# Attention followed by a squared-ReLU feed-forward layer: the tokens of layer one's second half in reverse order, the ReLU moved to layer two's reads, and x's sums moved up in GpSimd's queue

## The chip, the cores and the metric

One core of one Trainium2 chip. The metric is the device time of one launch in microseconds (us), median of several runs.

## The reference

Attention over 8 batches and 12 heads (448 positions, 64 wide) with RMS-normalised q and k gives x, 3584 tokens by 768. Then the feed-forward layer:

```python
h = x @ w_in                 # 3584 x 768 by 768 x 2048: layer one
r = np.maximum(h, 0.0)
g = s * (r * r) + b
return (g @ w_out).astype(np.float32)    # 3584 x 2048 by 2048 x 768: layer two
```

w_in and w_out come as 64-bit floats and are turned into 32-bit ones on the chip. All outputs are 32-bit floats.

## The kernel before

The kernel has three parts that follow each other: attention (up to 548 us in the profile), layer one (548 to 1028 us) and layer two (from 1033 us). The program writes the order of each engine's instructions by hand: what is emitted first on an engine runs first on it, and an instruction that waits holds up all that is behind it on its engine. The sync engine's queue (SP) issues nearly all DMAs of the two layers, in the same way. Data dependences, and buffers that are used again, are guarded by semaphores that the framework puts in.

Both layers multiply by a seven-product scheme on two-by-two blocks (`MUL`), and each 32-bit operand is split in a rounded part and a remainder, so that one product takes three multiplies. So each operand needs *sums* of its four quarters (`s_sums` for x, `sums_right` for w_out, `g_sums` for g: additions on GpSimd, POOL in the profile) and a *split* (`split`: a copy on ScalarE, ACT, then a subtraction on VectorE, DVE, lines 149 and 151).

**Layer one.** A block is one group of 512 tokens (seven groups, `NG`) times one of eight column groups of w_in (`q`). Four column groups fit in SBUF at a time, so there are two halves: `runs` lists seven groups of tokens with columns 0 to 3, then seven with columns 4 to 7. A run is four blocks (i = 0 to 3), and there are 14 runs, 56 blocks. A block is 63 multiplies into four PSUM banks (`ffn_in`, line 478). As there are eight banks, a block can start when the block two before it has been read out. x's three tiles (k = 0, 1, 2) of the next run are made during the present one:

- `s_load`: a load from DRAM of k = 0 and 1 in block i = 0, of k = 2 in block i = 2, into two buffers in turn;
- `s_sums` (lines 137 to 139): k = 0 and 1 in block i = 1, k = 2 in block i = 2;
- `s_split`: k = 0 in block i = 1, the two others in block i = 3.

In each block the order of emission is: the block's multiplies, `s_load`, the load of a piece of w_out (`convert_out`), `rectify` of the block before, the rest of the w_out conversion that was begun a block earlier (`finish(x)`: four DVE instructions, one on ACT, and, every second time, three sums on POOL and a store to `w_d`), and then `steps`: x's sums and splits, and loads and splits of weights. `rectify` adds up the seven products: four ACT copies and eight DVE additions out of PSUM (lines 487 to 492), a ReLU on ACT over 128 x 1024 (line 522), and a store to `r_d`. The w_out pieces are put together in one buffer (`o9`), free again when its store to `w_d` has landed.

At the turn between the halves (blocks 24 to 32) the columns 4 to 7 of w_in are loaded (`tin_load`, six buffers) and split (`tin_split`, 12 times, the subtraction on POOL), while x's tiles of token group 0 are loaded and made once more.

**Layer two.** 112 rounds of 21 multiplies (`multiply`, line 643). Each round reads a piece of `r_d` back (`g_load`), squares it on ACT (line 605, 128 x 512), scales it on DVE, makes the sums on POOL and DVE, and splits it (ACT line 627, DVE line 628), two to three rounds ahead of its multiplies. Eight rounds make 256 tokens, and `combine` adds the products up. The first rounds also need w_out's last splits (`tout_load`, `tout_split`). Between the layers the last block is rectified.

Of the kernel before, what the change touches and what calls it, by code (L numbers as in the profile page):

```python
# [12 lines left out]
AF = mybir.ActivationFunctionType  # L13
# [32 lines left out]
def attention_then_relu2_ffn(  # L46
# [13 lines left out]
    V, S, G, T = nc.vector, nc.scalar, nc.gpsimd, nc.tensor  # L60
# [82 lines left out]
    def t_in(q):  # L143
        if q not in tin:
            tin[q] = wpool.tile([P, NK, 2, 7, P], F32R, tag=f"s{q % QUADS}", name=f"tin{q}")
        return tin[q]

    def split(to, of, E=V):
        S.copy(to[0], of)  # L149
        yield  # L150
        E.tensor_tensor(to[1], of, to[0].bitcast(F32), ALU.subtract)  # L151
# [284 lines left out]
    s9s, sns = {}, {}  # L436

    def s_load(n):
        g, k = divmod(n, NK)
        g %= NG  # L440
        t = s9s[n] = pools["s9", n % 2].tile([P, 9, 2 * P], F32, tag="s9", name=f"s9_{n}")
        t0 = TG * g
        while t0 < TG * (g + 1):
            b, off = divmod(t0, SEQ)
            w = min(TG * (g + 1) - t0, SEQ - off)
            o = t0 - TG * g
            nc.sync.dma_start(
                four(t, 2 * P)[:, :, o : o + w],
                x_d[b][2 * k : 2 * k + 2, :, off : off + w].rearrange("f p t -> p f t"),
            )  # L450
            t0 += w

    def s_sums(n):
        sums_right(s9s[n], G)
# [7 lines left out]
    def finish(g):  # L462
        for _ in g:
            pass
# [2 lines left out]

    hs, rfirst = {}, []

    def ffn_in(r, q):  # L470

        banks = hs[q] = [psum(f"h{r}_{q}_{i}") for i in range(4)]
        for k in range(NK):
            w, x = t_in(q)[:, k], sns[NK * r + k]
            for j, (sa, tb) in enumerate(MUL):
                to = banks[j // 2][0][:, j % 2 * 2 * P : (j % 2 + 1) * 2 * P]
                for n, (lw, lx) in enumerate(((0, 0), (1, 0), (0, 1))):
                    T.matmul(  # L478
                        to, w[:, lw, sa], x[:, lx, tb],
                        start=k == n == 0 and j % 2 == 0, stop=k == NK - 1 and n == 2,  # L480
                        skip_group_check=True,
                    )
# [23 lines left out]
    def rectify(r, g, q):  # L506

        banks = hs.pop(q)
        if r == 0 or (r, q) == (1, 0):
            if not rfirst:  # L510
                rfirst.append(pools["t4"].tile([P, QUADS + 1, 2 * TG], F32, tag="t0", name="rfirst"))
            rt = rfirst[0][:, QUADS * r + q]
        else:
            rt = lp.tile([P, 2 * TG], F32, tag="uz", bufs=4, name=f"r{g}_{q}")
        c = [rt[:, i * 2 * P : (i + 1) * 2 * P] for i in range(4)]

        def part(j):
            return banks[j // 2][0][:, j % 2 * 2 * P : (j % 2 + 1) * 2 * P]

        add_up(c[3], c[2], c[1], c[0], part)  # L520
        free.extend(bank for _, bank in banks)
        S.activation(rt, rt, AF.Relu)  # L522
        nc.sync.dma_start(
            r_d[q][g].rearrange("f p t -> p f t"), rt.rearrange("p (f t) -> p f t", f=2)
        )
# [13 lines left out]
    def tin_split(n):  # L539
        q, k = divmod(n, NK)  # L540
        to = t_in(QUADS + q)
        return split((to[:, k, 0], to[:, k, 1]), staged[0][:, n % 6], G)

    touts = {}

# [41 lines left out]
    PAIRS = NT // (2 * P)  # L587
    ROUNDS = NM * PAIRS

    raws, g9s, ghs = {}, {}, {}  # L590

    def g_load(x):
        if x >= ROUNDS:
            return
        p, m = divmod(x, NM)
        raw = raws[x] = pools["g"].tile([P, 2, 2 * P], F32, tag="raw2", bufs=3, name=f"raw2_{x}")
        g, o = p // 2, p % 2 * 2 * P
        nc.sync.dma_start(raw, r_d[m][g][:, :, o : o + 2 * P].rearrange("f p t -> p f t"))

    def g_sums(x):  # L600
        if x >= ROUNDS:
            return
        raw = raws.pop(x)
        g9 = g9s[x] = pools["g"].tile([P, 9, P], F32, tag="g9", bufs=2, name=f"g9_{x}")
        S.activation(raw, raw, AF.Square)
        V.tensor_scalar(four(g9, P), raw, sb_s, sb_b, ALU.mult, ALU.add)  # L606
        G.tensor_tensor(  # L607
            g9[:, 2:4], g9[:, 0:2], g9[:, 7:8].broadcast_to([P, 2, P]), ALU.add
        )
        V.tensor_tensor(g9[:, 4], g9[:, 1], g9[:, 8], ALU.add)  # L610
        G.tensor_tensor(g9[:, 5:7], g9[:, 0:9:8], g9[:, 1:8:6], ALU.subtract)  # L611
# [40 lines left out]
    def combine(p):  # L652
        ot = ots[p] = pools["w9"].tile([P, 2, DM], F32, tag="w9", bufs=2, name=f"ot{p}")

        def done(j, h):
            if p == PAIRS - 1:
                t0, c = (2 * p + j) * P, slice(h * HALF, (h + 1) * HALF)
                nc.sync.dma_start(out[t0 : t0 + P, c], ot[:, j, c])

        add_up(  # L660
            ot[:, 1, HALF:], ot[:, 1, :HALF], ot[:, 0, HALF:], ot[:, 0, :HALF],
            lambda j: ms[p, j][0][:, :HALF], done,
        )
        free.extend(ms.pop((p, j))[1] for j in range(7))

    def store(p):
        ot = ots.pop(p)
        for j in range(2):
            t0 = (2 * p + j) * P
            nc.sync.dma_start(out[t0 : t0 + P, :], ot[:, j])  # L670

    def pool(stack, name, side, **of):
# [4 lines left out]
    with tc.manual_schedule(engines=ORDERED):  # L677
# [21 lines left out]
            tc.tile_pool(name="ps", bufs=1, space=PSUM, reuse_waits="tile")  # L699
        )  # L700
        todo = list(range(4 * NM))
        runs = [(g, q0) for q0 in (0, QUADS) for g in range(NG)]
        blocks = [(r, g, q0 + i) for r, (g, q0) in enumerate(runs) for i in range(QUADS)]
        nb = len(blocks)

        def steps(n):

            r, g, q = blocks[n]
            i = q % QUADS
            s0 = NK * (r + 1)  # L710
            if r + 1 < len(runs):
                if i == 1:
                    s_sums(s0)
                    s_sums(s0 + 1)
                    finish(s_split(s0))
                elif i == 2:
                    s_sums(s0 + 2)
                elif i == 3:
                    finish(s_split(s0 + 1))
                    finish(s_split(s0 + 2))  # L720
            b = n - (NG - 1) * QUADS
            if -2 <= b <= 0:
                for k in range(2):
                    tin_load(2 * (b + 2) + k)
            if 0 < b <= QUADS:
                for k in range(NK):
                    finish(tin_split(NK * (b - 1) + k))
                    tin_load(NK * (b + 1) + k)
            if n == nb - 14:
                tout_load(0)  # L730
                tout_load(1)
            if n == nb - 13:
                finish(tout_split(0))
                finish(tout_split(1))
            b = n - (nb - QUADS)
            if b == 0:
                tout_load(2)
                tout_load(3)
            elif b > 0:
                for k in (2 * b, 2 * b + 1):  # L740
                    finish(tout_split(k))
                    tout_load(k + 2)

        for n, (r, g, q) in enumerate(blocks):
            ffn_in(r, q)
            i = q % QUADS
            if r + 1 < len(runs):
                if i == 0:
                    s_load(NK * (r + 1))
                    s_load(NK * (r + 1) + 1)  # L750
                elif i == 2:
                    s_load(NK * (r + 1) + 2)
            begun_, fresh = begun[:], []
            begun.clear()
            if n >= 2 and todo and i != 2 and not 24 <= n < 29:
                c = convert_out(todo.pop(0))
                next(c)
                fresh.append(c)
            if n:
                rectify(*blocks[n - 1])  # L760
            for u in range(3 * n, 3 * n + 3):
                if u < 20:
                    slot(NSLOT + 2 + u)
            for x in begun_:
                finish(x)
            begun.extend(fresh)
            steps(n)
            if n == nb - QUADS - 1:
                assert not todo and not begun
                late.close()  # L770
                pools["g"] = pool(ctx, "gpool", "left")
                for x in range(3):
                    g_load(x)
            if n == nb - 3:
                g_sums(0)
                g_sums(1)
            if n == nb - 2:
                g_load(3)
                g_load(4)
        g_split(0)  # L780
        mid.close()
        pools["t"] = pool(ctx, "tpool", "right")
        g_split(1)
        g_sums(2)
        rectify(*blocks[-1])
        for k in (8, 9):
            finish(tout_split(k))
            tout_load(k + 2)
# [61 lines left out]
```

## Time and profile before

| | |
|---|---|
| median of 3 runs | 1466.35 us (1465.26 to 1466.78) |
| profiled execution | 1465.44 us |
| its span | 1463.7 us |
| PE, busy share of the span | 93% |
| DVE / ACT / POOL | 67% / 52% / 57% |
| mean granted TensorE clock | 0.972 |

The profile was taken of one execution; the span goes from its first to its last instruction, and 1.74 us lie outside of it. PE is TensorE's matrix multiply. A busy PE means that a multiply is under way; in a gap between multiplies it waits for an engine or a transfer. "<-" in a row names what ended the wait just before.

### The profile page before, as it was taken

What the parts mean: (1) busy time and instruction counts of PE and PEld (TensorE: products, weight loads), DVE (VectorE), ACT (ScalarE), POOL (GpSimd) and SP (SyncE); (2) the same over time, 40 slices, a digit from 0 to 9 for tenths busy, and PEclk for the clock granted to TensorE, in tenths of its full rate; (3) what the DMA queues carried; (4) which work ended last, traced back from release to release, by engine and by line L of the source; (5) the groups of instructions that cost most, each with busy time, mean ns of one, the idle gap of its engine ahead of it and who ended that gap; (6) DMA issues with size and microseconds to landing.
All of it is one profiled execution on the core that took longest, in us unless ns stands there. A gap on an engine that the chain in (4) does not pass through costs nothing.

```text
span 1463.7 us, 26101 instructions
## 1 busy us (share of the span) xinstructions
PE 1357.6 (93%) x9760; PEld 1079.9 (74%) x9760; DVE 975.4 (67%) x1534; ACT 766.7 (52%) x1132; POOL 839.2 (57%) x731
## 2 busy tenths in 40 slices
PE   2699999999999999899998899989699999999999
PEld 2344444444444439899988798989699999999998
DVE  3467777766666624676754676777786777677765
ACT  3367777776666653444445444445554444444443
POOL 6357989887878535444458435342265465546553
PEclk6799999999999999999999999999799999999999
DMA  7578888889998635465665465645632233223221
GB/s 199 157 197 227 252 230 231 252 235 265 253 266 255 179 88 158 152 201 168 196 208 180 143 196 172 209 153 203 222 132 96 85 122 95 94 87 123 94 94 65
DMA packets 172366, 253.71 MB, mean 173 GB/s; under 512 B 54544, under 2 KB 122832, under 8 KB 172240
## 3 DMA queue, kind: packets, MB, share of 16 engines
q1 hardware_dynamic: 165904, 231.86, 51.6%
q10 hardware_dynamic: 6336, 20.19, 5.2%
q8 instruction: 76, 1.25, 0.4%
q14 instruction: 50, 0.41, 0.1%
HBM read 183.06 MB, written 68.76 MB: 172 GB/s over the span
## 4 chain that ended last, share of the span: by engine, by line
PE 53%; issue 12%; DMA 11%; POOL 9%; DVE 8%; ACT 4%; SPq 2%; ACTq 0%; POOLq 0%; DVEq 0%
PE m L643 26%; PE av L293 8%; PE st L272 7%; PE av L300 4%; PE sh L243 4%; DVE r L487 3%; PE h L478 3%; DMA s<-x_d 2%; POOL s L139 2%; PE st L276 2%; DVE s L151 2%; DMA to<-w_d 2%; ACT s L149 2%; POOL s L138 1%; POOL s L137 1%
## 5 line engine op out<-in xcount | busy, mean ns | idle before, releaser
L478 PE MATMUL h<-s,tin 128*128 128x256 f32 x3528 | 440.2, 287 | 40.4 <-DVE r L487 19.5
L478 PEld LDWEIGHTS h<-s,tin 128*128 128x128 f32 x3528 | 431.0, 192 | 50.5 <-DVE r L487 24.7
L643 PE MATMUL m<-tout,gh 128*128 128x384 f32 x1568 | 406.3, 340 | 7.4 <-ACT gh L627 7.1
L252 DVE TENSOR_REDUCE nmx<-sh 112x2 fp32r<-112x896 f32 x192 | 209.1, 1091 | 142.4 <-PE sh L243 141.3
L643 PEld LDWEIGHTS m<-tout,gh 128*128 128x128 f32 x1568 | 288.7, 191 | 8.7 <-ACT gh L627 7.7
L643 PE MATMUL m<-tout,gl 128*128 128x384 f32 x784 | 267.2, 341 | 4.7 <-DVE gl L628 4.7
L283 ACT ACTIVATE e<-st 128x896 f32<-128x896 f32 x192 | 177.1, 922 | 118.7 <-PE st L276 118.4
L607 POOL TENSOR_TENSOR g<-g 128x256 f32<-128x256 f32 x112 | 94.5, 844 | 225.1 <-DVE g L606 225.1
L627 ACT CAST gh<-g 128x896 fp32r<-128x896 f32 x112 | 105.4, 942 | 174.7 <-POOL g L611 97.8
L628 DVE TENSOR_TENSOR gl<-g,gh 128x896 fp32r<-128x896 f32 x112 | 137.2, 1226 | 65.0 <-ACT gh L627 64.9
L272 PE MATMUL st<-kqv 64*128 64x448 f32 x768 | 179.9, 545 | 0.0
L151 DVE TENSOR_TENSOR s<-s,s 128x1792 fp32r<-128x1792 f32 x42 | 87.5, 2105 | 130.9 <-ACT s L149 122.7
L293 PE MATMUL av<-e,kqv 128*32 128x448 f32 x1536 | 164.4, 545 | 9.5 <-ACT uz L316 7.0
L643 PEld LDWEIGHTS m<-tout,gl 128*128 128x128 f32 x784 | 149.5, 191 | 6.5 <-DVE gl L628 6.5
L487 DVE TENSOR_TENSOR r<-r,h 128x256 f32<-128x256 f32 x408 | 139.5, 412 | 18.1 <-ACT r L491 17.8
L229 POOL TENSOR_TENSOR kqv<-kqv,rb 128x448 f32<-128x448 f32 x95 | 124.2, 1324 | 38.8 <-ACT kqv L225 13.9
L522 ACT ACTIVATE r<-r 128x1024 f32<-128x1024 f32 x51 | 54.1, 1061 | 173.9 <-DVE r L487 173.9
L202 POOL TENSOR_TENSOR ri<-ri,mhalf 128x14 f32<-128x14 f32 x48 | 141.7, 2951 | 4.0
L243 PEld LDWEIGHTS sh<-kr 64*112 64x112 f32 x384 | 54.3, 277 | 121.4 <-issue 29.5
L276 PE MATMUL st<-shq,row 64*128 64x448 f32 x384 | 139.6, 719 | 3.5 <-DMA shq<-nmx 3.5
L611 POOL TENSOR_TENSOR g<-g 128x256 f32<-128x256 f32 x112 | 133.4, 1191 | 0.0
L243 PE MATMUL sh<-kr 64*112 64x448 f32 x384 | 91.7, 474 | 35.4 <-ACT kr L234 25.3
(78 smaller groups left out, 1584.8 us busy)
## 6 DMA issues: line engine op xcount, KB each, us to landing
kqv<-in_dram SPq DMA_DIRECT2D x48, 704.0 KB
raw<-r_d SPq DMA_DIRECT2D x112, 256.0 KB
r_d<-r SPq DMA_DIRECT2D x51, 512.0 KB
rb<-i_d SPq DMA_DIRECT2D x96, 224.0 KB
raw<-in_dram ACTq DMA_DIRECT2D x44, 448.0 KB
w64i<-in_dram SPq DMA_DIRECT2D x24, 512.0 KB
w64o<-in_dram SPq DMA_DIRECT2D x32, 384.0 KB
uz<-z_d SPq DMA_DIRECT2D x96, 112.0 KB
```

The costliest lines, as they stand in the source:

```text
L202: G.tensor_tensor(ri, ri, mhalf[:, :n], ALU.pow)
L243: T.matmul(sh[:QC, j, :SEQ], t[d, 1].rearrange("k (p c) -> k c p", c=NQ)[:, c], t[d, 0], start=True, stop=True,)
L252: V.tensor_reduce(out=nmxs[p][:, :, c : c + 1], in_=shs.pop(i)[:QC, :, :SEQ], op=ALU.max, axis=AX.X, negate=True,)
L272: T.matmul(st[:, j, :SEQ], t[d, 0, k0 : k0 + P], t[d, 1], start=True, stop=False)
L276: T.matmul(st[:, j, :SEQ], row[d], shq[p % 3][d], start=False, stop=True)
L283: S.activation(e, sts.pop(i)[:, :, :SEQ], AF.Exp)
L293: T.matmul(t[n * Q : (n + 1) * Q, 0, :SEQ], x[:, 2 * g + h, j, m * Q : (m + 1) * Q], e[h][:, j], start=g + h == 0, stop=g + h == 2,)
L478: T.matmul(to, w[:, lw, sa], x[:, lx, tb], start=k == n == 0 and j % 2 == 0, stop=k == NK - 1 and n == 2, skip_group_check=True,)
L487: V.tensor_tensor(to, a, part(j), op_)
L611: G.tensor_tensor(g9[:, 5:7], g9[:, 0:9:8], g9[:, 1:8:6], ALU.subtract)
L628: V.tensor_tensor(gl, g9[:, 1:8], gh.bitcast(F32), ALU.subtract)
L643: T.matmul(to, g[:, sa], w, start=m == 0 and n == 0, stop=m == NM - 1 and n == 2,)
```

## The change

- `runs` takes the second half's token groups backwards (6 to 0), so the last run of the first half and the first of the second use the same tokens. x's tiles are kept from the one to the other (`first_s`, `fresh_x`): 13 sets of x's tiles are made instead of 14, and none during run 6. Layer two and the stores to `out` take the tokens backwards too (`tokens`).
- `rectify` has no ReLU any more; `g_sums` applies it to the 128 x 512 tile that layer two has read, ahead of the square, 112 times.
- `steps` is cut in two: `sums` (x's sums on POOL) stands ahead of `rectify` and of the rest of the w_out conversion; `parts` (splits, weights) stays behind them.
- The subtraction of `tin_split` is on DVE for k = 0 and 1, and on POOL for k = 2 alone.
- One more conversion of w_out is begun in block 28 instead of a later one (`24 <= n < 28`).
- The last block's `rectify` stands ahead of `g_split(1)` and `g_sums(2)`.

```diff
-        g, k = divmod(n, NK)
-        g %= NG
+        u, k = divmod(n, NK)
+        g = min(u, 2 * NG - 2 - u)
...
+    def first_s(r):
+        return NK * (r if r < NG else r - 1)
...
-            w, x = t_in(q)[:, k], sns[NK * r + k]
+            w, x = t_in(q)[:, k], sns[first_s(r) + k]
...
-        S.activation(rt, rt, AF.Relu)
...
-        return split((to[:, k, 0], to[:, k, 1]), staged[0][:, n % 6], G)
+        return split((to[:, k, 0], to[:, k, 1]), staged[0][:, n % 6], G if k == 2 else V)
...
+    def tokens(p):
+        return 2 * (NG - 1 - p // 2) + p % 2
...
+        S.activation(raw, raw, AF.Relu)
         S.activation(raw, raw, AF.Square)
...
-        runs = [(g, q0) for q0 in (0, QUADS) for g in range(NG)]
+        runs = [(g, 0) for g in range(NG)] + [(g, QUADS) for g in reversed(range(NG))]
...
+        def fresh_x(r):
+            return r + 1 < len(runs) and r != NG - 1
+
+        def sums(n):
+
+            r, _, q = blocks[n]
+            if fresh_x(r):
+                for k in {1: (0, 1), 2: (2,)}.get(q % QUADS, ()):
+                    s_sums(first_s(r + 1) + k)
+
+        def parts(n):
+
+            r, _, q = blocks[n]
+            if fresh_x(r):
+                for k in {1: (0,), 3: (1, 2)}.get(q % QUADS, ()):
+                    finish(s_split(first_s(r + 1) + k))
...
-            if n >= 2 and todo and i != 2 and not 24 <= n < 29:
+            if n >= 2 and todo and i != 2 and not 24 <= n < 28:
...
+            sums(n)
             if n:
                 rectify(*blocks[n - 1])
...
-            for x in begun_:
+            for x in last:
                 finish(x)
-            begun.extend(fresh)
-            steps(n)
+            begun.extend(next_)
+            parts(n)
...
+        rectify(*blocks[-1])
         g_split(1)
         g_sums(2)
-        rectify(*blocks[-1])
```

## Rows read from the trace of the kernel before

**Rows 1.** The page's first part: busy us (share of span), instructions.

```profile
PE 1357.6 (93%) x9760; PEld 1079.9 (74%) x9760; DVE 975.4 (67%) x1534; ACT 766.7 (52%) x1132; POOL 839.2 (57%) x731
```

**Rows 2.** Windows, layer one's multiplies by run: stretch, length, busy (count), granted clock.

```profile
548.12:581.58 33.46, 32.54 (x252) 32.33 (x253) 0.92 0.52 153
581.58:617.02 35.44, 31.24 (x254) 30.20 (x253) 1.00 0.51 169
...
684.52:715.77 31.25, 30.82 (x254) 30.20 (x253) 1.00 0.52 171
...
783.21:827.97 44.76, 33.83 (x254) 32.39 (x253) 0.92 0.42 141
...
925.79:964.84 39.05, 32.74 (x254) 31.71 (x253) 0.96 0.62 206
...
692.69:707.64 14.95, 14.95 (x128) 14.95 (x127) 1.00 0.56 193
sum 494.47, PE 455.17 PEld 445.95; mean PE 30.34 PEld 29.73
```

**Rows 3.** Waits in layer one: who waited for whom, us, times, longest.

```profile
POOL o L137 <- DVE o L118: 174.5, 15, 17.7
ACT r L522 <- DVE r L487: 170.1, 50, 5.6
DVE s L151 <- ACT s L149: 101.1, 23, 8.9
ACT s L149 <- POOL s L139: 60.2, 16, 6.5
```

**Rows 4.** Timeline of POOL, run 3: start, us, line, tiles, idle before.

```profile
665.23 1.00 POOL L137 TENSOR_TENSOR o<-o 128x384 f32<-128x384 f32 x1 [13.88 <-DVE o L118]
...
667.71 1.28 POOL L137 TENSOR_TENSOR s<-s 128x512 f32<-128x512 f32 x1
...
672.83 3.06 POOL L139 TENSOR_TENSOR s<-s 128x512 f32<-128x512 f32 x1
```

**Rows 5.** Timeline of DVE, runs 3 and 4.

```profile
660.22 2.74 DVE L487 TENSOR_TENSOR r<-r,h 128x256 f32<-128x256 f32 x8 [0.25 <-ACT r L491]
...
672.69 2.06 DVE L151 TENSOR_TENSOR s<-s,s 128x1792 fp32r<-128x1792 f32 x1 [7.59 <-ACT s L149]
...
685.78 3.96 DVE L151 TENSOR_TENSOR s<-s,s 128x1792 fp32r<-128x1792 f32 x2 [2.71 <-ACT s L149]
```

**Rows 6.** Timeline of PE: run 3, the run after the turn, layer two's start.

```profile
675.13 12.32 PE L478 MATMUL h<-s,tin 128*128 128x256 f32 x86 [1.85 <-DVE r L487]
...
818.35 12.55 PE L478 MATMUL h<-s,tin 128*128 128x256 f32 x86 [6.50 <-DVE r L487]
...
1033.51 1.01 PE L643 MATMUL m<-tout,gh 128*128 128x384 f32 x2 [5.88 <-ACT gh L627]
```

**Rows 7.** Timeline of POOL at the turn.

```profile
784.39 1.28 POOL L137 TENSOR_TENSOR s<-s 128x512 f32<-128x512 f32 x1 [5.95 <-DMA s<-x_d]
...
789.34 20.47 POOL L151 TENSOR_TENSOR tin<-staged,tin 128x896 fp32r<-128x896 f32 x9
```

**Rows 8.** Timeline, a load of x: its issue on SP, its first use.

```profile
674.77 0.87 SPq L447 DMA_DIRECT2D s<-x_d  x2
...
678.45 1.56 POOL L137 TENSOR_TENSOR s<-s 128x512 f32<-128x512 f32 x1 [2.56 <-DMA s<-x_d]
```

**Rows 9.** Lines by form, layer one, then two: busy, mean ns, idle before, releasers.

```profile
L522 ACT ACTIVATE r<-r 128x1024 f32<-128x1024 f32 x49 | 52.0, 1061 | 166.7 <-DVE r L487 166.7
...
L627 ACT CAST gh<-g 128x896 fp32r<-128x896 f32 x105 | 98.9, 942 | 172.1 <-POOL g L611 95.2 <-PE m L643 74.8 <-DVE g L610 2.1
...
L605 ACT ACTIVATE raw<-raw 128x512 f32<-128x512 f32 x103 | 64.7, 628 | 0.0
```

**Rows 10.** Windows, all engines (PE, PEld, DVE, ACT, POOL busy): run 4; layer two.

```profile
684.52:715.77 31.25, 30.82 (x254) 30.20 (x253) 24.52 (x47) 14.19 (x26) 13.08 (x13) 1.00 0.52 171
...
1085.00:1463.00 378.00, 375.15 (x2148) 374.82 (x2146) 265.26 (x405) 168.94 (x252) 198.82 (x201) 1.00 0.30 98
```

More of the change, by code (lines that the diff above doesn't have):

```diff
@@ L596, in g_load @@
         raw = raws[x] = pools["g"].tile([P, 2, 2 * P], F32, tag="raw2", bufs=3, name=f"raw2_{x}")
-        g, o = p // 2, p % 2 * 2 * P
+        g, o = tokens(p) // 2, p % 2 * 2 * P
         nc.sync.dma_start(raw, r_d[m][g][:, :, o : o + 2 * P].rearrange("f p t -> p f t"))
@@ L656, in done @@
             if p == PAIRS - 1:
-                t0, c = (2 * p + j) * P, slice(h * HALF, (h + 1) * HALF)
+                t0, c = (2 * tokens(p) + j) * P, slice(h * HALF, (h + 1) * HALF)
                 nc.sync.dma_start(out[t0 : t0 + P, c], ot[:, j, c])
@@ L668, in store @@
         for j in range(2):
-            t0 = (2 * p + j) * P
+            t0 = (2 * tokens(p) + j) * P
             nc.sync.dma_start(out[t0 : t0 + P, :], ot[:, j])
@@ L701, in attention_then_relu2_ffn @@
         todo = list(range(4 * NM))
-        runs = [(g, q0) for q0 in (0, QUADS) for g in range(NG)]
+        runs = [(g, 0) for g in range(NG)] + [(g, QUADS) for g in reversed(range(NG))]
         blocks = [(r, g, q0 + i) for r, (g, q0) in enumerate(runs) for i in range(QUADS)]
         nb = len(blocks)
[L706 to L720, printed above, removed]
+        def fresh_x(r):
[10 more added lines that the diff above has]
+                    finish(s_split(first_s(r + 1) + k))
             b = n - (NG - 1) * QUADS
@@ L746, in attention_then_relu2_ffn @@
             i = q % QUADS
[L747 to L753, printed above, removed]
+            if fresh_x(r):
+                for k in {0: (0, 1), 2: (2,)}.get(i, ()):
+                    s_load(first_s(r + 1) + k)
+            last, next_ = begun[:], []
             begun.clear()
-            if n >= 2 and todo and i != 2 and not 24 <= n < 29:
+            if n >= 2 and todo and i != 2 and not 24 <= n < 28:
                 c = convert_out(todo.pop(0))
                 next(c)
-                fresh.append(c)
+                next_.append(c)
+            sums(n)
             if n:
```

## The prediction

> **What bounds the kernel now.** I read the page's first part, then windows cut by run, then the waits of layer one, and last the timelines of the places found. PE is busy for 93% of the span [rows 1], so only its gaps can be won, and the windows say where they are. Two blocks that run freely take 14.95 us for 126 multiplies [rows 2], so a run of four costs 29.90 us and layer one's 14 runs 418.6. They take 494.47 - 14.95 = 479.5. So 60.9 us are lost in layer one. In layer two from 1085 us on PE is busy for 375.15 of 378.00 us [rows 10]: nothing is to be had there.
>
> The loss has three forms. (a) Run 7, at the turn, takes 44.76 us [rows 2]. POOL is then busy with nine subtractions of w_in's splits for 20.47 us in one go [rows 7], x's sums stand behind them, and PE waits 6.50 us in one place [rows 6]. (b) Five runs (1, 3, 5, 9, 11; the first and the last stand in the rows, 35.44 and 39.05) take 177.9 us together. In them w_out's sums come up in block i = 1, ahead of x's on POOL. POOL sits idle 13.88 us for DVE's w_out words, and only then makes x's sums, from 667.71 us [rows 4], though x's loads were issued a block earlier and need some 3.7 us [rows 8]. ACT and DVE wait for them in order, DVE for 7.59 us [rows 5], so the next rectify is late and PE waits for its banks, 1.85 us [rows 6], and longer in run 11. The waits show the same chain as totals: POOL for DVE 174.5, DVE for ACT 101.1, ACT for POOL 60.2 us [rows 3]. (c) The seven other runs have 479.5 - 33.5 - 44.8 - 177.9 = 223.4 us, 31.9 each; run 4 is the best with 31.25. There DVE stands idle 2.71 us in block i = 3 [rows 5], behind the ReLU of 1.06 us [rows 9] and the split's copy, because ACT sits in front of the ReLU until DVE has finished the additions (170.1 us in all [rows 3]). PE then meets an x tile that is late.
>
> **The change, part by part.** All against the profiled execution's 1465.44 us (span 1463.7 and 1.74 around it), which is 0.91 under the median.
>
> *The turn.* Run 6 makes no x: three loads, nine POOL sums (3.3 us a tile: 1.28, the shorter middle one and 1.28 [rows 4, 7]), three ACT copies and three DVE subtractions of 2.06 us [rows 5] go. Eight of the twelve subtractions of w_in go from POOL (20.47 / 9 = 2.27 us each [rows 7]) to DVE. DVE's price for 128 x 896 isn't in the rows: half of 2.06 us for twice the size is 1.03, and POOL's own 2.27 bounds it above. I take 1.1, nearest to DVE's own row. So DVE gets 8.8 us (8.2 to 18.2) and loses 6.2, in blocks 25 to 28, which hold no w_out conversion but one begun in block 28. Its load of 24.52 us a run [rows 10] leaves 5.4, which hides the rest; uncovered it would cost 3 (12 at the upper bound). Run 7 should cost what the best run costs: 44.76 - 31.25 = **-13.5**. The tokens' reversal itself moves addresses alone: each half's first group is still the one that layer two reads first.
>
> *x's sums ahead on POOL.* In the five runs, loads issued in block 0 have landed when block 1 starts (issue to first use took 3.7 us [rows 8]), so x's sums run while DVE is still at the rectify and the conversion. Then nothing sets these runs apart: 177.9 - 5 x 31.25 = **-21.6**. What is added is a wait of w_out's sums behind x's: in block 2 behind a load that is itself issued only when k = 0's split has freed the buffer. Behind those sums on POOL stands nothing of x until the next run; behind the store to `w_d` stand SP's next loads and, by the single `o9`, DVE's next conversion. A conversion held for 1 to 2 us lies in DVE's spare 5.4; that cover gone, it delays the next rectify by the same.
>
> *ReLU out of rectify.* 56 instructions of 1.06 us leave ACT, 59 us, and the order behind them: the split's copy no longer waits for DVE's additions, so the 2.71 us of DVE idle time goes in each run that makes x. PE has of it at most run 4's excess, 1.35 us, times the 12 runs besides 0 and 7: 0 to -16. I take half, **-8**: the path then is DVE's own work. The seven runs of (c) lie 223.4 - 218.7 = 4.7 above run 4; **-3** of it goes the same way. The store to `r_d` leaves earlier, and what stands behind it on SP.
>
> *ReLU into layer two.* 112 instructions over 128 x 512. The square of that shape takes 0.63 us [rows 9]; half of 1.06 is the floor (0.53), 1.06 the ceiling. I take 0.63, 70 us (59 to 119) in all. ACT is busy 168.94 of 378 us there, and before each gh copy idle 172.1 / 105 = 1.64 us, more than half of it for POOL and the rest for PE [rows 9]: the ReLU stands in that. **0**; some 8 if the first ten rounds, where gh is late for PE, took it all.
>
> *The join.* PE waits 5.88 us at layer two's start [rows 6]; ReLUs and late rectifies lie in front of that on ACT, and transfers of w_out's pieces too. Between 0 and -5.9: I take **-3**.
>
> *Contention.* In the trace a POOL sum of 1.28 us takes 3.06 while a DVE subtraction runs beside it [rows 4, 5], 1.78 more; it ends 1.1 us after the subtraction, which itself was no longer than elsewhere. So they don't share, one waits. x's sums will now lie beside w_out's DVE work and beside splits. I take 0.5 us for each of the 12 runs, **+6** (0 to all of POOL's 13.08 us a run [rows 10], which is the second rival).
> The Trainium skill has this as a rule (SBUF — State Buffer, "Who interferes with whom"): VectorE and GpSimd have one pair of ports in common, an exclusive lock for the whole instruction. The trace agrees: 3.06 against 1.28 us. It speaks against putting more POOL work beside DVE's two-input instructions.
>
> Sum: -13.5 - 21.6 - 8 - 3 + 0 - 3 + 6 = -43.1. 1465.44 - 43.1 = 1422.3 profiled, 1423 as a median.
>
> **The rivals.**
> *The wait moves.* The turn is won, and the rest ends elsewhere: x's sums wait for their loads, w_out's store comes late and holds DVE's conversion, or the DVE, at 24.5 of 29.9 us, is the pace itself. For it: POOL already waited 2.56 and 5.95 us for x [rows 7, 8]. Against: run 4 ran at 31.25 with the same work. Price: the turn's 13.5 and half of 21.6, without the other gains and without the contention, -24 (-12 to -30): 1442, 1436 to 1454.
> *The lock, slower than before.* x's sums come to lie on DVE's two-input work (words of w_out, splits), each blocks the other, and DVE becomes the pace. The 12 runs last (177.9 + 223.4) / 12 = 33.4 us now, DVE works 24.5 of them; with the turn won (1.1 us a run), it decides from 33.4 + 1.1 - 24.5 = 10.0 us of blocking a run, three quarters of POOL's 13.08. At 12 us: 12 x (36.5 - 33.4) - 13.5 = +24, so 1490. For it: the 3.06 us row. Against: DVE's additions, the largest part of its work (2.74 us a block, 11 of 24.5 a run [rows 5]), read PSUM and kept their length, so there is room beside them.
> That is also what the Trainium skill's rule, as cited above, makes of it.
> *ACT bounds layer two.* The added ReLU isn't hidden: +70 - 43 = +27, 1493. Against: 168.94 + 65 = 234 of 378 us.
> *No effect of the order.* In runs whose w_out sums fall in block 0, POOL's order at x's sums is the old one; that is in the forecast, which takes nothing from it.
>
> **The numbers.** Forecast 74%; the wait moves 15%; lock 6%; ACT in layer two 2%; gains and costs cancel 3%. A difference below 0.2% (3 us) can't be told from no change. So faster 0.89, same 0.03, slower 0.08. The forecast's own range is 1405 (PE nearly free in layer one: 12 runs at 30.2, the join won) to 1436. The range reaches up into the first rival: 1406 to 1446.
>
> **What would show it.** Run 7 at 31 to 32 us with no long POOL stretch; runs 1, 3, 5, 9, 11 as long as their neighbours, 30 to 31.5; POOL's w_out sums now behind x's, and their wait for DVE still large but harmless; no DVE idle time of 2.7 us ahead of the splits in block 3; layer two from 1085 us on as long as before. Wrong it would be if PE still waits for DVE's rectify twice a run, if DVE's rows of the conversion grow beyond 2 us a block more, or if layer two's gh copies come to end PE's waits.

## The result, and the profile after

The changed kernel takes **1423.1 us** (median of 4 runs, 1421.84 to 1425.28) where the kernel before took 1466.57 us beside it on the same chip: a ratio of 0.9706, 95% interval 0.969 to 0.9723. The forecast was 1423. The profiled execution took 1423.74 us, its span 1422.0.

The page's first part, after (busy us, share of span, instructions), to be read against [rows 1]:

```profile
PE 1345.4 (95%) x9760; PEld 1070.7 (75%) x9760; DVE 1002.1 (70%) x1539; ACT 780.2 (55%) x1185; POOL 838.6 (59%) x714
```

PE's busy time fell by 12.2 us for the same multiplies and its idle time by the rest. Part of that is PE's clock: before, the mean granted clock was 0.92 to 0.96 in runs 3, 6, 7 and 11, that is, partly at the lower level (1.2 GHz) and otherwise at 2.4 GHz (in run 7 it fell in the gap of 6.50 us [rows 6]); after, behind run 0, it was so in run 12 alone (0.95). The share that is missing to 1.00, times the length of these runs, makes 8.6 us before and 1.7 after: by this estimate some 7 us of layer one's gain are the clock, which the prediction had inside its run lengths without naming it. DVE works 26.7 us more than before, though it got only five instructions more, 2.6 us by the forecast: most of the difference is rows that got longer, and that comes back below.

Of the span's 41.7 us, layer one gave 35.7 (479.5 to 443.9) and the stretch from its end to layer two's tenth round 2.5 (58.2 to 55.7). The rounds behind give 0.1 (377.8 to 377.7). The remaining 3.4 us lie in attention, which the change doesn't touch; its end lay between 542.7 and 553.3 us in the profiles of all kernels here, so this is taken for scatter.

Layer one run by run, in us, each from the windows of one profiled execution (the other kernels' follow below; run 0 came out between 32.6 and 38.5 us and isn't read):

| run | 0 | 1 | 2 | 3 | 4 | 5 | 6 | 7 | 8 | 9 | 10 | 11 | 12 | 13 | sum |
|---|---|---|---|---|---|---|---|---|---|---|---|---|---|---|---|
| before | 33.5 | 35.4 | 32.2 | 35.3 | 31.3 | 33.9 | 33.5 | 44.8 | 31.4 | 34.2 | 32.2 | 39.1 | 31.3 | 31.5 | 479.5 |
| after | 35.3 | 29.9 | 29.9 | 32.3 | 32.1 | 32.8 | 32.4 | 30.2 | 30.2 | 30.2 | 30.2 | 34.1 | 33.8 | 30.5 | 443.9 |

Windows of layer one's multiplies, after (stretch, length, PE and PEld busy with counts, granted clock, DMA share, GB/s): runs 1, 3, 7 and 11, and the sum of all.

```profile
579.97:609.88 29.91, 29.91 (x254) 29.91 (x253) 1.00 0.54 183
...
639.78:672.03 32.25, 30.91 (x254) 30.11 (x252) 1.00 0.61 207
...
769.24:799.48 30.24, 30.24 (x254) 30.24 (x253) 1.00 0.44 142
...
890.20:924.30 34.10, 31.98 (x254) 30.52 (x253) 1.00 0.53 175
...
sum 443.86, PE 431.12 PEld 425.21; mean PE 30.79 PEld 30.37
```

Run 1 has no gap. Run 7, the costliest before [rows 2], has none either: its length is its busy time. Run 11 still loses 4 us. Waits in layer one (who waited for whom, total us, times, longest):

```profile
ACT o L110 <- DMA w_d<-o: 76.5, 9, 11.7
POOL s L137 <- DMA s<-x_d: 63.7, 12, 9.5
POOL o L137 <- DVE o L118: 57.8, 11, 12.5
...
ACT s L149 <- POOL s L139: 24.3, 12, 5.2
DVE o L111 <- DMA w_d<-o: 21.4, 6, 3.9
...
DVE s L151 <- ACT s L149: 13.3, 9, 4.8
...
PE h L481 <- DVE r L490: 6.6, 5, 2.0
...
PE h L481 <- DVE s L151: 4.2, 4, 1.6
```

And PE's own two waits before:

```profile
PE h L478 <- DVE r L487: 19.5, 8, 6.5
PE h L478 <- DVE s L151: 18.4, 15, 1.7
```

PE waited 19.5 us for rectify's additions (line 487, now 490) and 18.4 us for the last step of x's splits (line 151); now it waits 6.6 and 4.2. The chain of [rows 3] is gone: DVE for ACT fell from 101.1 to 13.3 us, ACT for POOL from 60.2 to 24.3, POOL's wait ahead of w_out's sums from 174.5 to 57.8, and ACT's 170.1 us in front of the ReLU went with it. At the top are transfers now: w_out's store to `w_d`, which frees `o9` (76.5 us for ACT, 21.4 for DVE), and x's loads.

Where the rest of the loss begins shows around run 3. POOL, after (start, us, line, tiles, idle before):

```profile
636.97 1.01 POOL L137 TENSOR_TENSOR o<-o 128x384 f32<-128x384 f32 x1
637.95 2.38 POOL L138 TENSOR_TENSOR o<-o 128x192 f32<-128x192 f32 x1
640.28 2.79 POOL L139 TENSOR_TENSOR o<-o 128x384 f32<-128x384 f32 x1
```

SP, after:

```profile
643.10 0.33 SPq L587 DMA_DIRECT2D w_d<-o  x1
...
645.01 3.44 SPq L447 DMA_DIRECT2D s<-x_d  x4
...
648.50 0.46 SPq L573 DMA_DIRECT2D w64o<-in_dram  x1
```

DVE, then PE, after:

```profile
654.79 1.08 DVE L111 TENSOR_SCALAR o<-w64o 128x384 int32<-128x384 int32 x1 [1.69 <-DMA w64o<-in_dram]
...
668.31 0.36 DVE L111 TENSOR_SCALAR o<-w64o 128x384 int32<-128x384 int32 x1 [3.70 <-DMA w_d<-o]
```

```profile
553.67 117.04 PE L481 MATMUL h<-s,tin 128*128 128x256 f32 x964 [1.56 <-DVE s L151]
...
672.03 3.55 PE L481 MATMUL h<-s,tin 128*128 128x256 f32 x23 [1.32 <-DVE r L490]
```

PE runs 117 us without a gap, almost to the end of run 3. But w_out's three sums take from 636.97 to 643.07; in a kernel below, with nothing beside them, three such sums take 2.62 us. The store behind them leaves SP in that moment, and x's loads and the next w_out piece, emitted for the block that began at 639.78, stand behind it on SP until 645.01 and 648.50. DVE then waits 1.69 us for that piece and, a piece later, 3.70 us for the store to free `o9`. The rectify behind it is late, and PE waits at 672.03.

### The profile page after: what moved, and what is told of

It is laid out like the page before. It is cut to its first block, busy times and chain, and to the rows that moved or that the text cites. A ratio compares the mean times of both kernels' runs of the same rounds, so it can differ in the third digit from the quotient of the medians.

```text
span 1422.0 us, 25928 instructions
## 1 busy us (share of the span) xinstructions
PE 1345.4 (95%) x9760; PEld 1070.7 (75%) x9760; DVE 1002.1 (70%) x1539; ACT 780.2 (55%) x1185; POOL 838.6 (59%) x714
## 3 DMA queue, kind: packets, MB, share of 16 engines
q1 hardware_dynamic: 164272, 230.29, 52.5%
## 4 chain that ended last, share of the span: by engine, by line
PE 66%; DMA 11%; DVE 9%; issue 5%; POOL 5%; SPq 2%; ACT 2%; ACTq 0%; DVEq 0%; POOLq 0%
PE m L649 27%; PE h L481 12%; PE av L293 9%; PE st L272 8%; PE av L300 4%; PE sh L243 4%; PE st L276 2%; DMA w64o<-in_dram 2%; DMA to<-w_d 2%; DVE s L151 2%; DVE r L490 2%; DMA s<-x_d 1%; DMA i_d<-ri 1%; DMA kqv<-in_dram 1%; SPq L447 1%
## 5 line engine op out<-in xcount | busy, mean ns | idle before, releaser
L481 PE MATMUL h<-s,tin 128*128 128x256 f32 x3528 | 431.1, 284 | 13.8 <-DVE r L490 6.6
L481 PEld LDWEIGHTS h<-s,tin 128*128 128x128 f32 x3528 | 425.2, 190 | 20.4 <-DVE r L490 11.2
L229 POOL TENSOR_TENSOR kqv<-kqv,rb 128x448 f32<-128x448 f32 x95 | 125.1, 1332 | 32.7 <-ACT kqv L225 16.2
L137 POOL TENSOR_TENSOR s<-s 128x512 f32<-128x512 f32 x39 | 54.5, 1396 | 137.1 <-DMA s<-x_d 79.4
L243 PE MATMUL sh<-kr 64*112 64x448 f32 x384 | 92.2, 476 | 35.1 <-ACT kr L234 25.2
L151 DVE TENSOR_TENSOR s<-s,s 128x1792 fp32r<-128x1792 f32 x39 | 82.4, 2125 | 43.3 <-ACT s L149 35.1
```

The source lines that it names most:

```text
L243: T.matmul(sh[:QC, j, :SEQ], t[d, 1].rearrange("k (p c) -> k c p", c=NQ)[:, c], t[d, 0], start=True, stop=True,)
L481: T.matmul(to, w[:, lw, sa], x[:, lx, tb], start=k == n == 0 and j % 2 == 0, stop=k == NK - 1 and n == 2, skip_group_check=True,)
```

## The experiments

All times are medians; ratios are to the kernel before, run beside each, with their 95% intervals. Three kernels add one part to the kernel before, three take one part out of the changed one, one splits the turn, and five ask what bounds the changed kernel. That the last block's rectify stands further ahead was not run by itself: it is in none of the first three and in all the others. Differences in us are of medians; by the ratios they come out up to 3 us otherwise, as the kernel before itself moved between 1466.5 and 1468.2 us. Runs of layer one (us):

| kernel | 0 | 1 | 2 | 3 | 4 | 5 | 6 | 7 | 8 | 9 | 10 | 11 | 12 | 13 | sum |
|---|---|---|---|---|---|---|---|---|---|---|---|---|---|---|---|
| before + turn | 32.6 | 36.9 | 31.4 | 35.4 | 31.0 | 35.0 | 31.1 | 29.9 | 30.7 | 32.2 | 35.4 | 33.7 | 35.2 | 30.1 | 460.5 |
| before + x's sums ahead | 33.0 | 29.9 | 31.0 | 31.8 | 32.6 | 31.9 | 33.7 | 44.3 | 30.6 | 33.6 | 32.0 | 37.9 | 32.8 | 33.0 | 468.2 |
| before + ReLU on reads | 37.9 | 33.7 | 29.9 | 34.9 | 29.9 | 35.1 | 29.9 | 42.4 | 29.9 | 34.9 | 29.9 | 38.2 | 29.9 | 32.4 | 468.9 |
| after, forward again | 38.5 | 29.9 | 29.9 | 30.4 | 32.2 | 32.6 | 36.3 | 35.2 | 31.5 | 31.9 | 32.8 | 34.8 | 33.1 | 33.1 | 462.0 |
| after, sums behind | 33.5 | 35.3 | 30.2 | 36.1 | 30.2 | 34.7 | 29.9 | 29.9 | 29.9 | 29.9 | 34.9 | 32.3 | 35.5 | 30.1 | 452.5 |
| after, ReLU back | 33.3 | 29.9 | 30.6 | 31.9 | 35.9 | 29.9 | 31.9 | 29.9 | 29.9 | 32.2 | 31.9 | 36.4 | 31.9 | 30.8 | 446.3 |
| after, store later | 32.7 | 30.2 | 30.2 | 30.2 | 30.2 | 30.8 | 31.5 | 29.9 | 29.9 | 29.9 | 30.7 | 34.7 | 30.6 | 30.1 | 431.8 |
| after, no w_out sums | 33.4 | 29.9 | 29.9 | 29.9 | 29.9 | 29.9 | 29.9 | 29.9 | 29.9 | 29.9 | 29.9 | 29.9 | 29.9 | 30.1 | 422.3 |

**The turn alone** (kernel before with the turn's part: reversed tokens, x's tiles kept, the subtractions, and the conversion begun in block 28; the two lines that matter).

```diff
-        runs = [(g, q0) for q0 in (0, QUADS) for g in range(NG)]
+        runs = [(g, 0) for g in range(NG)] + [(g, QUADS) for g in reversed(range(NG))]
...
-        return split((to[:, k, 0], to[:, k, 1]), staged[0][:, n % 6], G)
+        return split((to[:, k, 0], to[:, k, 1]), staged[0][:, n % 6], G if k == 2 else V)
```

> The kernel before with the turn's part alone: tokens reversed, x's tiles kept, w_in's subtractions of k = 0 and 1 on DVE, one conversion begun in block 28. ReLU in rectify, POOL's order and the end of layer one as before. Theory (the parts of the change add up; the turn's own term was put at 13.5 us, and going forward cost the changed kernel 18): 1447 to 1454 us. Rival (reversal pays only once the ReLU and POOL's order are gone): 1457 to 1464 us.

1447.96 us, ratio 0.9872 (0.9843 to 0.9901): some 19 us, where the forecast had 13.5. Windows of this kernel, runs 5 and 7:

```profile
715.67:750.67 35.00, 32.01 (x254) 31.60 (x253) 0.95 0.63 209
...
781.72:811.62 29.90, 29.90 (x254) 29.90 (x253) 1.00 0.54 174
```

Run 7 falls by 14.9 us and run 6 by 2.4; run 5, which makes x behind w_out's sums, keeps its loss.

**The turn taken back** (changed kernel): forward order, 14 sets of x; the subtractions of `tin_split` stay on DVE.

```diff
-        runs = [(g, 0) for g in range(NG)] + [(g, QUADS) for g in reversed(range(NG))]
+        runs = [(g, q0) for q0 in (0, QUADS) for g in range(NG)]
...
-            return r + 1 < len(runs) and r != NG - 1
+            return r + 1 < len(runs)
```

> The changed kernel with the second half's tokens forwards again, so that x's tiles are made anew at the turn (14 sets); w_in's subtractions stay on DVE for k = 0 and 1. Theory (making x anew at the turn is what cost the turn its time): +8 to +14, 1431 to 1437 us, lost in runs 6 and 7. Rival (the subtractions that POOL did were the cost, and they are still gone): 1422 to 1427 us.

1441.7 us, ratio 0.9842 (0.9814 to 0.987): 18.6 us lost, more than the theory's upper bound of 14. Its windows of runs 6 and 7:

```profile
738.26:774.57 36.31, 32.96 (x254) 32.00 (x253) 0.95 0.79 270
774.57:809.72 35.15, 32.30 (x254) 31.68 (x253) 0.95 0.43 142
```

Run 7 is not back at 44.8, as the subtractions no longer hold POOL; instead run 6, in which x is made beside the loads of w_in (270 GB/s), loses 4 us, run 7 loses 5, and runs 8 to 10 and 13 lose 1 to 3 us each. The 9 us of runs 6 and 7 are what the theory named; it had nothing for the later runs.

**Only the subtractions back on POOL** (changed kernel).

```diff
-        return split((to[:, k, 0], to[:, k, 1]), staged[0][:, n % 6], G if k == 2 else V)
+        return split((to[:, k, 0], to[:, k, 1]), staged[0][:, n % 6], G)
```

> The changed kernel with all twelve subtractions of w_in's splits on POOL again; tokens still reversed. Theory (POOL has no x to make in blocks 24 to 27, so three subtractions of 2.1 us fit in each block): 0 to +4, 1422 to 1427 us, although POOL has one long stretch again. Rival (that long stretch holds up x's sums for run 8 and was the turn's cost): +8 to +14, 1431 to 1437 us.

1425.43 us, ratio 0.9726 (0.9694 to 0.9758), not told apart from the changed kernel. With no x to make, the subtractions may lie on either engine. With x made and the subtractions on DVE (the kernel above) run 7 took 35.2 us, with both on POOL 44.8: so most of what cost run 7 its 14.9 us was x's sums *behind* the subtractions on POOL, and 5 us of it making x at all.

**x's sums ahead, alone** (kernel before).

```diff
-                    s_sums(s0)
-                    s_sums(s0 + 1)
...
-                elif i == 2:
-                    s_sums(s0 + 2)
...
+            if r + 1 < len(runs):
+                for k in {1: (0, 1), 2: (2,)}.get(i, ()):
+                    s_sums(NK * (r + 1) + k)
             if n:
                 rectify(*blocks[n - 1])
```

> The kernel before with x's sums ahead of rectify and of the w_out conversion in POOL's queue, and nothing else. Theory of the prediction (the order alone sets five runs apart): 21.6 less 6 us of contention, 1447 to 1455 us, with no run above 33 us but 0 and 7. Rival (order and ReLU remove the same waits; alone each does most of what both do, so that taking one back cost the changed kernel only 6 to 9 us): the same time here, but then the ReLU alone gives as much. If both rivals fail (the two need each other): 1460 us or more.

1455.59 us, ratio 0.992 (0.9892 to 0.9948): 12 us, half of the 21.6 forecast and just above the theory's range. Windows of this kernel, runs 1, 4 and 11:

```profile
580.83:610.74 29.91, 29.91 (x254) 29.91 (x253) 1.00 0.54 177
...
673.57:706.15 32.58, 30.96 (x254) 30.14 (x253) 1.00 0.48 159
...
912.28:950.19 37.91, 32.94 (x254) 32.45 (x253) 0.91 0.65 212
```

The mechanism is right in run 1 (35.4 to 29.9), and in PE's own waits: over layer one PE waits 7.6 us for rectify's additions where it waited 19.5, and still 17.8 for the last step of x's splits where it waited 18.4. But runs 9 and 11 stay at 33.6 and 37.9, and runs 4, 12 and 13, which had nothing to lose, lengthen by 1.3 to 1.5 us.

**x's sums behind again** (changed kernel: `sums(n)` moved to just before `parts(n)`).

> The changed kernel with x's sums again behind rectify and the w_out conversion in POOL's queue. Theory (POOL's order alone sets five runs apart, worth 21.6 us less some 6 us of contention): 1435 to 1445 us, with POOL's w_out sums ahead of x's and PE waiting for rectify in every other run. Rival (with the ReLU gone, ACT and DVE reach the conversion early enough that POOL's order no longer matters): 1422 to 1428 us.

1429.2 us, ratio 0.9762 (0.9729 to 0.9795): 6 us lost, between the theory and the rival. In its profile layer one loses 8.6 us and the stretch from there to layer two's tenth round gives 3.8 back. Its windows of runs 3 and 4:

```profile
641.72:677.83 36.11, 32.52 (x254) 31.68 (x253) 0.95 0.54 181
677.83:708.07 30.24, 30.24 (x254) 30.24 (x253) 1.00 0.57 185
```

Runs 1, 3, 5 and 10 lose 2 to 5 us each again, but the runs between them have no gap, and in the changed kernel runs 4 and 6 had lost 2 us each. Lines by form, this kernel (count, busy us, mean ns, idle us before and its releasers):

```profile
L113 DVE SCALAR_TENSOR_TENSOR o<-w64o,o 128x384 int32<-128x384 int32 x32 | 20.0, 625 | 1.1
...
L137 POOL TENSOR_TENSOR o<-o 128x384 f32<-128x384 f32 x16 | 16.2, 1015 | 171.2 <-DVE o L118 171.2
```

And the changed kernel:

```profile
L113 DVE SCALAR_TENSOR_TENSOR o<-w64o,o 128x384 int32<-128x384 int32 x32 | 25.9, 808 | 1.1
...
L137 POOL TENSOR_TENSOR o<-o 128x384 f32<-128x384 f32 x16 | 26.5, 1654 | 57.8 <-DVE o L118 57.8
```

With x's sums ahead, POOL's work lies beside DVE's conversion, and both get longer: DVE's two-input instruction from 0.63 to 0.81 us, POOL's sum from 1.02 to 1.65. The Trainium skill's rule in "SBUF — State Buffer", section "Who interferes with whom" (an exclusive lock on the ports that the two engines have in common), agrees in direction with these rows; what it costs PE, the last experiments ask.

**ReLU on reads, alone** (kernel before).

```diff
-        S.activation(rt, rt, AF.Relu)
...
+        S.activation(raw, raw, AF.Relu)
         S.activation(raw, raw, AF.Square)
```

> The kernel before with the ReLU moved to layer two's reads, and nothing else. Theory of the prediction (8 + 3 us in layer one, up to 3 at the join): 1452 to 1458 us, the five runs with w_out's sums ahead still some 3 us longer than the others. Rival (the ReLU holds up the same chain as POOL's order, so it alone shortens those five runs too): 1442 to 1451 us.

1449.39 us, ratio 0.9871 (0.9853 to 0.9889): 19 us, in the rival's range but not by its mechanism. Windows of this kernel, runs 2 to 4:

```profile
618.08:647.98 29.90, 29.90 (x254) 29.90 (x253) 1.00 0.59 189
647.98:682.86 34.88, 32.21 (x254) 31.60 (x253) 0.95 0.53 178
682.86:712.77 29.91, 29.91 (x254) 29.91 (x253) 1.00 0.58 187
```

The runs with x's sums behind w_out's (1, 3, 5, 9, 11) stay at 33.7 to 38.2. The six even runs from 2 to 12, in which POOL's order at x's sums is the same as with them ahead, fall to 29.90, every one (191.9 to 179.4 us together). There ACT stood in front of the ReLU with the split's copy behind it [rows 3, 5]; now PE waits 7.4 us for the last step of x's splits where it waited 18.4 (and 4.4 for the copy ahead of it, 1.2 before), and still 19.1 for rectify where it waited 19.5. So each of the two parts takes away most of one of PE's two waits. In this profile (1450.07 us) layer one is 10.6 us shorter than before, 15.0 without run 0, and the stretch behind it to layer two's tenth round 3.2 us: near the 11 and 3 that were forecast. Of the rest 1.6 us lie in attention, and what is left of the 19 us is in the medians alone.

**ReLU back in rectify** (changed kernel).

```diff
+        S.activation(rt, rt, AF.Relu)
...
-        S.activation(raw, raw, AF.Relu)
```

> The changed kernel with the ReLU back in rectify (128 x 1024, 56 times) and out of layer two's reads. Theory (the ReLU held the split's copy behind DVE's additions, worth 8 + 3 us): 1434 us, 1429 to 1440, with DVE idle some 2.7 us ahead of the splits in block 3 again. Rival (DVE's own work and the lock set the pace, the ReLU stood in idle time): 1420 to 1426 us.

1432.44 us, ratio 0.9776 (0.9742 to 0.981): 9.3 us lost, in the theory's range but not where the theory put it. In the profile, 8.7 us longer than the changed kernel's, 2.4 are in layer one, 3.7 between its end and layer two's tenth round, and 2.6 in attention, which this edit doesn't touch. The ReLU's own wait is back in layer one, as PE waits 12.3 us for the last step of x's splits (4.2 in the changed kernel); but PE's wait for rectify fell from 6.6 to 1.1 us, and the two nearly cancel. Why rectify comes earlier there was not pursued.

**Two ReLUs in layer two** (changed kernel: the ReLU on the read tile done twice).

> The changed kernel with the ReLU of layer two's reads done twice (the second changes nothing): 0.63 us more of ACT a round, 70 us in all. Prediction's theory (ACT idled 1.64 us a round ahead of the gh copy and took one ReLU into it; a second fits too): layer two from round 10 on as long as before, 377 to 379 us, in all 1423 to 1428 us, the first rounds a few us later. Rival (one ReLU used up the slack): 5 us or more in the rounds from 10 on, up to 70.

1426.67 us, ratio 0.9721 (0.9684 to 0.9758); the rounds from the tenth on last 377.7 us, as in the changed kernel. Windows of layer two (PE, PEld, DVE, ACT, POOL busy, clock, DMA share, GB/s), changed kernel:

```profile
1044.00:1422.00 378.00, 374.59 (x2145) 374.26 (x2143) 266.25 (x405) 231.65 (x351) 198.41 (x200) 1.00 0.31 97
```

With two ReLUs:

```profile
1048.00:1422.00 374.00, 374.00 (x2143) 374.00 (x2142) 267.77 (x404) 293.82 (x450) 209.91 (x201) 1.00 0.31 97
```

ACT goes from 168.94 us [rows 10] to 231.65 to 293.82, and PE stays full: what is added on ACT is taken from its idle time.

**What bounds the changed kernel.** First, the w_out loads ahead of x's loads on SP (the block that calls `next(c)` moved ahead of `s_load`).

> The changed kernel with the load of the next w_out piece issued ahead of x's loads in each block, on SP. Theory of what is left in layer one (in runs 3 to 6 and 11 to 13 SP holds the w_out load behind an x load that waits for its buffer; the conversion then waits for that load, 52.5 us on ACT and 18.2 on DVE, and rectify behind it): 1413 to 1419 us, those waits gone. Rival (what is left is the lock between POOL and DVE, or the store to w_d): 1421 to 1426 us.

1427.77 us, ratio 0.9724 (0.9699 to 0.9749): no gain. But the waits that the theory wanted gone only shrank, from 52.5 and 18.2 us to 38.3 and 11.1, and POOL waited longer for x's loads (94.3 us, some 63 in the changed kernel). So the edit shows that this order is no cure, not what those waits cost. Then the store to `w_d` issued a block later (two where i = 2), behind x's loads:

```diff
+            while stores and stores[0][0] <= n:
+                finish(stores.pop(0)[1])
...
-                finish(x)
+                for _ in range(5):
+                    next(x, None)
+                stores.append((n + (2 if i == 2 else 1), x))
```

> The changed kernel with w_out's store to w_d issued one block later (two from block i = 2), so behind the next x loads in SP's queue. Theory of what is left in layer one (w_out's sums are now behind x's on POOL, their store waits for them, 75 us in all, and holds x's loads behind it on SP): 1412 to 1420 us, the store's wait ahead of x's loads gone, runs 3 to 6 and 11 to 13 near 30.5 us. Rival (POOL and DVE in each other's way at the SBUF port set the pace): 1421 to 1427 us. It can turn slower where the conversion, by its single buffer, waits for the later store.

**1415.88 us** (1411.11 to 1417.68), ratio 0.964 (0.961 to 0.9671): in the theory's range, with SP's wait ahead of the store down from 126.8 us to 28.1 (below) and runs 3 to 6, 12 and 13 at 30.1 to 31.5 us; run 11 stays at 34.7. This is the fastest of the kernels that leave nothing out; its interval lies wholly under the changed kernel's. Third, the store issued by GpSimd (`G.dma_start` instead of `nc.sync.dma_start`):

> The changed kernel with w_out's store to w_d issued from POOL's queue, behind the sums that it waits for, so that SP never waits for it. Theory (the store on SP holds up x's loads): 1412 to 1420 us. Rival (the port lock sets the pace): 1421 to 1427, or slower if POOL's own issuing takes it long.

1428.63 us, ratio 0.9725 (0.9692 to 0.9759): no gain, against the theory. SP is free of the wait, and POOL waits 29.5 us for x's loads, as little as with the store later (32.1). But each issue takes 0.57 us of POOL, the store lands 5.4 us after it (median), and DVE waits more, not less, ahead of the conversion (70.1 us against 50.3); PE waits 11.1 us for rectify (6.6 in the changed kernel, 1.6 with the store later). So SP's wait is not by itself the price. Fourth, no sums of w_out on POOL, with one copy on ACT in their place; this leaves out w_out's sums:

```diff
-            sums_right(t, G)
+            S.copy(t[:, 6], t[:, 1])
```

> The changed kernel without w_out's three sums on POOL (a short ACT copy fills the one part that nothing else writes, so layer two gets wrong sums of w_out). 16 x 2.6 us leave POOL, and the store waits for DVE alone. Both theories give a gain; their sizes differ. Port lock (POOL's 3.9 us a run of w_out's sums, and what they hold up on DVE): 1410 to 1417 us, with DVE's conversion and splits back at 0.56 and 2.0 us. Store on SP: the same time as with the store issued later.

1407.4 us, ratio 0.9585 (0.955 to 0.962), lower than both ranges. Its windows of runs 3 and 11, and the sum:

```profile
643.88:673.78 29.90, 29.90 (x254) 29.90 (x253) 1.00 0.57 187
...
883.11:913.02 29.91, 29.91 (x254) 29.91 (x253) 1.00 0.59 192
...
sum 422.34, PE 421.25 PEld 420.85; mean PE 30.09 PEld 30.06
```

Every run behind the first has no gap. Lines by form, this kernel:

```profile
L113 DVE SCALAR_TENSOR_TENSOR o<-w64o,o 128x384 int32<-128x384 int32 x32 | 25.2, 789 | 1.1
```

DVE's row is as long as in the changed kernel (0.79 against 0.81 us; 0.56 was expected) and PE has no gap, so that lengthening by itself costs PE nothing here. Two things went together: POOL's sums and what waits for them. SP's waits ahead of the store (who waited for whom, total us, times, longest), in the changed kernel, with the store later, and without the sums:

```profile
SPq L587 <- POOL o L139: 75.0, 16, 7.9
...
SPq L587 <- DVE o L118: 51.8, 16, 6.9
```

```profile
SPq L587 <- POOL o L139: 20.8, 11, 2.6
...
SPq L587 <- DVE o L118: 7.3, 5, 1.7
```

```profile
SPq L587 <- ACT o L585: 47.0, 16, 5.3
```

That is 126.8, 28.1 and 47.0 us, while the layer-one sums are 443.9, 431.8 and 422.3: the shortest layer one does not have the shortest wait on SP. What is least without the sums is the wait for `o9`: ACT and DVE wait 9.6 and 0.4 us for the store to `w_d` to land, where they wait 76.5 and 21.4 in the changed kernel and 126.0 and 24.4 with the store later. So what is left of the loss behind run 0 hangs on w_out's sums on POOL: that is shown. Which of the things that wait for them is the price (the store on SP, `o9`, or POOL's own time) is not: the late store speaks for SP, the store on POOL's queue against it. With the store later, run 11 keeps 34.7 us; that run is half of what still separates the two.

## Why the prediction was right, point by point

The sum was right to a microsecond; its terms were not. By the medians three gains were off by 5 to 10 us each, in both directions.

- **The turn, forecast -13.5.** Right in mechanism: run 7 fell from 44.76 to 30.24 us, and where POOL had nine subtractions in one stretch of 20.47 us [rows 7], x's sums now stand behind single ones, as POOL's timeline after shows:

```profile
765.22 2.54 POOL L151 TENSOR_TENSOR tin<-staged,tin 128x896 fp32r<-128x896 f32 x1 [3.32 <-ACT tin L149]
...
774.26 2.16 POOL L137 TENSOR_TENSOR s<-s 128x512 f32<-128x512 f32 x1
```

  Too small: alone it gives 19 us, and undone it costs 18.6. The step that failed was to price run 7 alone against the best run; run 6, which no longer makes x, gains too. Moving the subtractions to DVE, costed at 8.8 us of DVE time and measured at 12.5 (eight of 1.57 us), is immaterial.
- **x's sums ahead, forecast -21.6.** Right in mechanism in runs 1, 3 and 5, too large in size: alone it gives 12 us, undone it costs 6. "Then nothing sets these runs apart" failed: in the kernel with this part alone the five runs went from 177.9 to 165.2 us, not to 156.3, because runs 9 and 11 keep their loss; and runs 4, 12 and 13 lengthened. In the changed kernel runs 3, 5 and 11 take 32.3, 32.8 and 34.1 us, above the 30 to 31.5 that was named as a sign.
- **ReLU out of rectify, forecast -8 and -3.** Right in mechanism, and in size by its profile: alone it takes 10.6 us from layer one (15.0 without run 0) and 3.2 from the join, though the medians differ by 19. Wrong in place: of the twelve runs that were to share it, the six even ones gave 12.5 us and the other six nothing. I took half of run 4's excess, as "the path then is DVE's own work". Runs 2, 4, ... 12 went to 29.90 us, all of it, so DVE's work was not the path there; ACT standing in order in front of the ReLU was.
- **ReLU into layer two, forecast 0.** Right, and even a second one costs nothing from the tenth round on (377.7 us).
- **The join, forecast -3.** The stretch gave 2.5 us. At the first multiply PE still waits 5.44 us where it waited 5.88 [rows 6]: the copy it needs now stands behind a split of w_out that waits for its transfer. ACT at the join, after:

```profile
991.80 1.31 ACT L149 CAST tout<-to 128x1344 fp32r<-128x1344 f32 x1 [2.85 <-DMA to<-w_d]
993.02 0.93 ACT L633 CAST gh<-g 128x896 fp32r<-128x896 f32 x1
```

- **Contention, forecast +6.** The three parts' ratios multiply to 0.9667, together they give 0.9706: 5.7 us are lost by overlap, close to the term, but the intervals of the four ratios come to about 7 us together, so this is no more than an indication. (Layer one alone, in single profiles: 41.0 us for the three parts, 35.7 together.) Its form is not borne out. I had priced the lock between DVE and POOL; where their work lies side by side rows get longer, by about 0.5 us a piece of w_out on DVE and from 2.62 to 4.05 us for POOL's three sums, but without those sums DVE's rows stay long and PE has no gap. What PE pays for are those sums and what waits for them, by a path that is open.
- **The rivals.** "The wait moves" named that very chain ("w_out's store comes late and holds DVE's conversion"): the changed kernel's remaining loss hangs on w_out's sums and their store, but it left a gain of 43 us and not of 24. The lock as a new pace did not come: without w_out's sums PE has no gap beside the lengthened rows. ACT as the bound of layer two is refuted by the doubled ReLU.

So the mechanisms of the three parts were right, but that the total came out to a microsecond is luck: errors cancelled. 13.5, 21.6 and 11 us of gain were forecast, 46.1 together with 3 at the join and 6 of contention apart; measured alone the parts give 18.8, 11.7 and 18.9, 49.4 with the join in it, and together 43.

Open: whether a second `o9` would close the gap between the late store and the kernel without w_out's sums (not tried); why the store issued by POOL gains nothing where the later store on SP does; what moving the last block's rectify is worth; and what holds run 11.

## What to carry to other kernels

Where an in-order queue holds loads for one consumer behind a store that waits for another, look at the queue that issues, not only at the engines that compute: here the same store one block later gave 7 us. But a long wait on that queue is not yet a price, as the store on another queue gave nothing. When parts of a change lie side by side, price each alone and don't expect the plain sum; here three parts worth 19, 12 and 19 us gave 43. Look for the wait of the bound engine that each part takes away: two of them took most of one each. A longer row is not a cost until someone waits for its end.

## What was not expected of the hardware

PE has two paces for the same multiplies at the same granted clock of 1.00: a run of 252 multiplies takes 29.90 us or 30.24 us (118.7 or 120.0 ns each), for whole stretches. In the changed kernel runs 7 to 10 all take 30.24 with no gap, PE after:

```profile
741.66 151.47 PE L481 MATMUL h<-s,tin 128*128 128x256 f32 x1260 [1.34 <-DVE s L151]
```

Without w_out's sums the same four runs take 29.90 or 29.91, and with the turn alone run 7 does. The cause was not found; it is worth 0.3 us a run.
